# Ending the first tile's attention before the fifth pair begins, and queueing phi behind the preceding pair's minima

## The chip, the cores and the metric

The kernel runs on 1 core of a Trainium2 chip. The metric is device time in microseconds (us) of one execution, lower is better. The engines are PE (matrix products and transposes), DVE (VectorE), ACT (ScalarE), POOL (GpSimd) and SP (which issues the transfers). Each works through its own instructions strictly in order; an instruction waits at the head of its engine until what it needs is there.

## The reference

Attention with a memory branch, then two feed-forward layers, all in float32:

```python
scores = scale * q @ k.T                    # B=4, H=8, S=576, D=64, causal
a = softmax(scores);  local = a @ v
q_p = phi(q)                                # phi(x) = max(x, 0) + min(exp(x), 1)
mem_out = (q_p @ M_prev) / (q_p @ z_prev + 1e-6)
x = g * mem_out + (1 - g) * local           # g = sigmoid(beta), one value a head
x = x.reshape(2304, 512)
h = x @ w_in;  x = (h * sigmoid(1.702 * h)) @ w_out     # 512 -> 2048 -> 512
h = x @ w_in2; x = (h * clip(h + 3, 0, 6) / 6) @ w_out2
```

The feed-forward weights come as 64-bit floats and are turned into 32-bit ones on the chip.

## The kernel before

**Tiles and pairs.** The 2304 tokens are six tiles of 384 columns (`TILES`). Tile 0 is the first 384 rows of batch 0, tile 1 those of batch 1, tile 2 the last 192 rows of both, and so on. The eight heads go two at a time: a tile of one batch has four *pairs* (`NP` = 4), so pairs 0 to 3 make tile 0 and pairs 4 to 7 tile 1.

**Attention of a pair** has three parts. `scores(i)` multiplies q by k into PSUM (names `s`); behind it DVE takes the masked row minima (`masked_min`, L484), ACT the exponentials (`expo`, L489, names `p`), DVE the reciprocals of the row sums (L492, L493) and POOL scales the rows (`norm`, L497). `turn(i)` transposes p on PE (L439, names `t`) and ACT copies the result out (L584, names `pt`). `weigh(i)` multiplies by v (names `o`) and ACT copies the result into the tile's columns `x0` to `x3` (L736), one for each pair. Beside it goes the memory branch: `mem_prep(i)` makes phi of q (ACT L652, DVE L654 and L655), `mem_read(i)` multiplies it by the memory matrix (PE L409, names `mem`) and DVE scales that (L676 to L680, names `mw`, `mo`).

**The pipeline.** `attention` (L440 to L778) is one loop over steps: step i emits the scores of pair i, the transposes of pair i-1 and the product with v of pair i-2. A step therefore holds work of three pairs. The first steps run ahead of everything else with eight PSUM banks (the *prelude*, L864 to L871) until `attention` reports that tile 0 is complete, which it does in step 5. Pairs 4 and 5 belong to tile 1 but their scores are in that prelude. After it `pump` (L827, rate at L887) emits the steps of the next tile's attention between the matmuls of the feed-forward layer, with three banks.

**Feed-forward, layer 0, tile 0.** A tile has 16 blocks f = 0 to 15 (`moe`, L298): four products h (L342), a tanh on ACT (L281) and a product on DVE (L283, result `g`), and four products y (L313) of the same block one block later. Tile 0 takes its weights as whole float32 (`r0` to `r15`); later tiles split them in two (L344 to L347, L314 to L317).

**Weight conversion** (`conv_w`, L168). For each `r{f}`: DVE shift (L186), DVE xor (L191), ACT L195, for some f an absolute value (DVE L199 or ACT L197), ACT L201 and DVE L206, whose result h(f) and y(f) read. `KQ` sets how early in the prelude the first two conversions are emitted (L870).

**What sets the order.** A scheduler orders each engine's instructions from the order in which they are written, within the dependencies; the first instruction of a conversion is kept at its written place (L190), and a conversion follows the DVE and ACT work of an earlier feed-forward block (`after_gates`, L133). The queues of PE, DVE and ACT are thus fixed when the program is built.

Of the kernel before, what the change touches and what calls it, by code (L numbers as in the profile page):

```python
# [12 lines left out]
ALU = mybir.AluOpType  # L13
# [5 lines left out]
NP = H // 2  # L19
# [2 lines left out]
N0, N1 = 384, 192  # L22
NT = 384
PRE = 2
KQ = 39
CR = 8.5
OFF = 3
PG0 = (0.85, 0.55)
PG1 = 0.86
TB = 3  # L30
PB = 6
# [33 lines left out]
BIG = 3.4028234e38  # L65
MZ = 132
TILES = [
    [(0, 0)],
    [(1, 0)],
    [(0, 1), (1, 1)],  # L70
    [(2, 0)],
    [(3, 0)],
    [(2, 1), (3, 1)],
]
# [30 lines left out]
def attention_moe_kernel(ctx: ExitStack, tc: tile.TileContext, qk0, sk0, sk1, vm0, vm1, bb, w1, w2, out):  # L105
    nc = tc.nc
    PE, ACT, DVE, POOL, SP = nc.tensor, nc.scalar, nc.vector, nc.gpsimd, nc.sync
# [332 lines left out]

    def attention(ap):
        qk, vm, pp, pt, phi, mo = {}, {}, {}, {}, {}, {}
        gens, made = {}, {}
        norms = [0, 0]

        t4 = ap.tile([128, 2, 64], F32, tag="t4", bufs=1, name="t4")
# [26 lines left out]
        def load_vm(i):  # L473
            if not 0 <= i < NPAIR:
                return
            ti, si, b, g, p, _ = pairs[i]
            t = ap.tile([128, 5 * 128 + MZ], F32, tag="vm", bufs=2, name="vm")
            nv = (3, 5)[g]
            move(2, out=t[:, 0:nv * 128 + MZ], in_=(vm0, vm1)[g][b, p])
            vm[i] = (t[:, MZ:MZ + nv * 128].rearrange("p (j c) -> p j c", j=nv), t[:, 0:130])  # L480

        def masked_min(o, m, init, out):

            DVE.tensor_tensor_reduce(  # L484
                out=o, in0=o, in1=m, scale=-SCALE, scalar=init, op0=ALU.add, op1=ALU.min, accum_out=out
            )

# [14 lines left out]
        def scores(i):  # L502

            ti, si, b, g, p, _ = pairs[i]
            norms[1] = ti
            q, k = qk[i]
            st = ap.tile([128, 12], F32, tag="st", name="st")
            mx, su = st[:, 0:6], st[:, 6:12]

            def product(banks, blocks):  # L510

                mm = in_a_run(free(banks[0]) + free(banks[1]))
                for o0, o1, c0 in blocks:
                    for a in range(2):
                        h = slice(64 * a, 64 * a + 64)
                        mm(
                            banks[a][:, o0:o1], lhsT=q[h, c0:c0 + 128], rhs=k[h, 0:o1 - o0], start=True, stop=True
                        )

            def soft(s, cols, dst, c):  # L520

                jobs = [(a, c0, c1, c + a * len(cols) + x) for a in range(2) for x, (c0, c1) in enumerate(cols)]
                yield
                for a, c0, c1, k in jobs:
                    masked_min(s[a][:, c0:c1], mask[:, 512 - (c1 - c0):512], BIG, mx[:, k:k + 1])
                yield
                for a, c0, c1, k in jobs:
                    d = expo(dst[a][:, c0:c1], s[a][:, c0:c1], mx[:, k:k + 1], su[:, k:k + 1])
                    if c1 == cols[-1][1]:
                        has_read(s[a], d)  # L530
                yield
                inverse(su[:, c:c + len(jobs)])
                yield
                for a, c0, c1, k in jobs:
                    norm(dst[a][:, c0:c1], su[:, k:k + 1], omg[:, 2 * p + a:2 * p + a + 1])

            pp[i] = []
            if g == 0:
                parts = (((0, 128, 0), (128, 384, 128)), ((0, 384, 256),))
            else:  # L540
                parts = (((0, 512, 0),),)
            t = [[ap.tile([128, 512], F32, tag="p", bufs=PB, name="p") for _ in parts] for _ in range(2)]
            pp[i] = [tuple(x) for x in t]
            c = 0
            for x, blocks in enumerate(parts):
                s = [bank("s") for _ in range(2)]
                product(s, blocks)
                start(("s", i, x), soft(s, [(o0, o1) for o0, o1, _ in blocks], [t[a][x] for a in range(2)], c))
                c += 2 * len(blocks)
                yield  # L550
            if g == 1:
                t = ap.tile([128, 512], F32, tag="p", bufs=PB, name="p4")
                t2 = ap.tile([128, 64], F32, tag="p5", name="p5")
                pp[i].append((t, t2))
                s, s2 = bank("s4"), bank("s5")
                mm = in_a_run(free(s) + free(s2))
                for o, c0, c1 in ((s, 0, 512), (s2[:, 0:64], 512, 576)):
                    for a in range(2):
                        h = slice(64 * a, 64 * a + 64)
                        mm(o[h], lhsT=q[h, 128:N1], rhs=k[h, c0:c1], start=True, stop=True)  # L560

                def soft4(s=s, s2=s2, t=t, t2=t2):
                    yield
                    masked_min(s, mask[:, 0:1].to_broadcast([128, 512]), BIG, mx[:, 2:3])
                    masked_min(s2[:, 0:64], mask4, mx[:, 2:3], mx[:, 3:4])
                    yield
                    has_read(s, expo(t, s, mx[:, 3:4], su[:, 2:3]))
                    has_read(s2, expo(t2, s2[:, 0:64], mx[:, 3:4], su[:, 3:4]))
                    yield
                    DVE.tensor_tensor(out=su[:, 2:3], in0=su[:, 2:3], in1=su[:, 3:4], op=ALU.add)  # L570
                    inverse(su[:, 2:3])
                    yield
                    norm(t, su[:, 2:3], omp[:, p:p + 1])
                    norm(t2, su[:, 2:3], omp[:, p:p + 1])

                start(("s", i, 2), soft4())
                yield
# [66 lines left out]
        def mem_prep(i):  # L644

            ti, si, b, g, p, _ = pairs[i]
            n = (N0, N1)[g]
            e = ap.tile([128, NT], F32, tag="tmp", bufs=TB, name="phi")
            phi[i] = e
            r = qk.pop(i)[0]  # L650
            yield
            ACT.activation(out=e[:, 0:n], in_=r, func=AF.Exp)  # L652
            yield
            DVE.tensor_scalar(out=e[:, 0:n], in0=e[:, 0:n], scalar1=1.0, scalar2=None, op0=ALU.min)  # L654
            DVE.scalar_tensor_tensor(out=e[:, 0:n], in0=r, scalar=0.0, in1=e[:, 0:n], op0=ALU.max, op1=ALU.add)  # L655

        def mem_read(i):
# [88 lines left out]
                yield None  # L746

        def has(i):
            return 0 <= i < NPAIR

        nil = iter(())
        load_qk(0)
# [1 line left out]
        load_qk(1)  # L754
        load_w(W0)
        gs, gt, gw = {}, {}, {}
        for i in range(NPAIR + 2):
            if has(i):
                gs[i] = scores(i)
            if has(i - 1):  # L760
                gt[i - 1] = turn(i - 1)
            if has(i - 2):
                gw[i - 2] = weigh(i - 2)
            s, t, w = gs.pop(i, nil), gt.pop(i - 1, nil), gw.pop(i - 2, nil)
            for gen, n in (
                (s, 1), (t, 1), (w, 1), (s, 1), (t, 1), (w, 9), (s, 1), (t, 1), (s, 9),
            ):
                yield from chunks(gen, n)
            if has(i):
                start(("p", i), mem_prep(i))  # L770
                load_qk(i + 2)
            if has(i - 2) and pairs[i - 2][5]:
                need(("x", i - 2))
                yield pairs[i - 2][0]
            load_vm(i)
            if has(i - 1):
                yield from mem_read(i - 1)
            yield from chunks(t, 9)  # L778


    with ExitStack():
# [80 lines left out]
        with tc.tile_pool(name="ap", bufs=2) as ap:  # L862
            temps[:] = [ap, TWB[0]]
            att = state["att"] = attention(ap)  # L864
            banks[0] = 8
            for k, mark in enumerate(att):
                chains.step()
                if mark is not None:
                    break
                convert_to(min(PRE, int(PRE * k / KQ) + K0))  # L870
            convert_to(PRE)  # L871
            banks[0] = 3
            phase["behind"] = lambda: marks[-1 - SLACK] if len(marks) > SLACK else None
            qi, ti = 0, 0
            for layer, t, f in stream:
                if t != ti:
                    ti, qi = t, 0
                    if t == LAST:
                        break
                if qi == 0:  # L880
                    state["emitted"], state["done"] = 0, False
                qi += 1
                if ti == 0:
                    convert_to(min(NF, PRE + 1 + int(qi / CR)))
                if ti < 2 and 128 * ti + qi >= S2:
                    part_to(1 + (128 * ti + qi - S2) // SR)
                pump((qi - OFF) / (PG0[min(ti, 1)] * 128 / 36 if TILES[ti + 1][0][1] == 0 else PG1 * 128 / 57))  # L887

        with tc.tile_pool(name="x2p", bufs=2) as x2p:
            state["pool"] = x2p  # L890
# [68 lines left out]
```

## Time and profile before

| | |
|---|---|
| median of 3 runs | 1048.41 us (1048.25 to 1051.59) |
| span of the profiled execution | 1049.0 us |
| time of the profiled execution beside its span | none is recorded of its own; the span is 0.6 us over the median |
| PE busy | 1029.6 us, 98% |
| DVE, ACT, POOL busy | 467.4, 510.2, 293.7 us |

PE, DVE, ACT and POOL are the engines; a busy share is over the whole span. In a row of the timeline the first number is the start in us, the second the time that the row's instructions took together, and the bracket at the end is how long the engine stood idle just before, and which instruction released it. The prelude lasts to 44.5 us, tile 0 of the feed-forward layer to 162.2 us.

### The profile page before, as it was taken

How to read it: one execution, taken by the hardware profiler on the slowest of the kernel's cores; microseconds unless marked ns; L12 is line 12 of the kernel's file. 1: busy time of each engine (PE TensorE's matmuls, PEld its weight loads, DVE VectorE, ACT ScalarE, POOL GpSimd, SP SyncE). 2: the span in 40 equal slices, each digit the busy share in tenths (PEclk: the TensorE clock that was granted, in tenths of full speed). 3: DMA queues.
4: the chain of work that ended last, by engine and by line, in shares of the span. 5: the costliest groups of instructions: out<-in, count | busy, mean ns of one | idle time of the engine just before them, and what ended most of it. 6: DMA issues, size and time to landing. Idle time of an engine off the chain costs nothing.

```text
span 1049.0 us, 16113 instructions
## 1 busy us (share of the span) xinstructions
PE 1029.6 (98%) x6025; PEld 914.9 (87%) x6025; DVE 467.4 (45%) x1153; ACT 510.2 (49%) x1110; POOL 293.7 (28%) x346
## 2 busy tenths in 40 slices
PE   8899999999999999999999999999999999999998
PEld 5555558988888888898889999999999999999998
DVE  6977766666533343433443697971121211211110
ACT  5876746545634454433333778883232332332322
POOL 4522112333333332322222241332222222222221
PEclk8999999999999999999999999999999999999999
DMA  5864314332211021111100784001010010000000
GB/s 185 277 232 137 136 55 153 129 118 65 81 42 36 26 67 46 31 31 61 47 16 16 271 302 173 18 11 52 1 46 16 10 52 1 31 31 1 31 1 30
DMA packets 33885, 80.27 MB, mean 77 GB/s; under 512 B 4112, under 2 KB 13328, under 8 KB 33808
## 3 DMA queue, kind: packets, MB, share of 16 engines
q1 hardware_dynamic: 33808, 79.25, 22.4%
q8 instruction: 47, 0.77, 0.3%
q14 instruction: 30, 0.25, 0.1%
HBM read 61.41 MB, written 9.44 MB: 68 GB/s over the span
## 4 chain that ended last, share of the span: by engine, by line
PE 86%; DVE 6%; ACT 5%; issue 2%; DMA 1%; SPq 0%; POOL 0%; DVEq 0%; ACTq 0%
PE y L315 11%; PE h L344 11%; PE y L317 11%; PE y L316 11%; PE h L347 11%; PE h L346 11%; PE s L424 5%; PE o L424 5%; PE h L342 3%; PE y L313 3%; PE t L439 3%; ACT p L489 2%; PE mem L409 1%; DVE s L484 1%; DVE r L191 1%
## 5 line engine op out<-in xcount | busy, mean ns | idle before, releaser
L295 POOL TENSOR_TENSOR g<-t,g 128x384 fp32r<-128x384 f32 x173 | 185.2, 1071 | 481.6 <-ACT g L292 433.0
L344 PE MATMUL h<-xs,w 128*128 128x384 f32 x704 | 241.4, 343 | 1.6 <-DVE t L283 0.9
L315 PE MATMUL y<-g,w 128*128 128x384 f32 x704 | 237.2, 337 | 0.5 <-ACT g L292 0.5
L316 PE MATMUL y<-g,w 128*128 128x384 f32 x704 | 236.3, 336 | 0.0
L346 PE MATMUL h<-xs,w 128*128 128x384 f32 x704 | 236.0, 335 | 0.3 <-DVE w L228 0.3
L347 PE MATMUL h<-xs,w 128*128 128x384 f32 x704 | 236.0, 336 | 0.0
L317 PE MATMUL y<-g,w 128*128 128x384 f32 x704 | 223.6, 338 | 0.0
L287 DVE SCALAR_TENSOR_TENSOR t<-t,h 128x384 f32<-128x384 f32 x96 | 53.0, 553 | 275.5 <-ACT t L285 275.4
L344 PEld LDWEIGHTS h<-xs,w 128*128 128x128 f32 x704 | 132.3, 188 | 10.1 <-issue 5.2
L285 ACT ACTIVATE t<-h,three 128x384 f32<-128x384 f32 x96 | 55.6, 580 | 170.2 <-PE h L347 170.1
L497 POOL TENSOR_SCALAR p<-p,st,omg 128x128 f32<-128x128 f32 (+3 forms) x128 | 85.8, 683 | 186.3 <-DVE st L493 122.1
L317 PEld LDWEIGHTS y<-g,w 128*128 128x128 f32 x704 | 130.4, 188 | 5.6 <-issue 4.9
L315 PEld LDWEIGHTS y<-g,w 128*128 128x128 f32 x704 | 132.2, 188 | 2.8 <-issue 1.3
L292 ACT CAST g<-t 128x384 fp32r<-128x384 f32 x176 | 90.1, 514 | 90.9 <-DVE t L287 49.3
L346 PEld LDWEIGHTS h<-xs,w 128*128 128x128 f32 x704 | 132.4, 188 | 0.7 <-DVE w L228 0.5
L316 PEld LDWEIGHTS y<-g,w 128*128 128x128 f32 x704 | 132.2, 188 | 0.7 <-issue 0.5
L347 PEld LDWEIGHTS h<-xs,w 128*128 128x128 f32 x704 | 132.2, 188 | 0.5 <-issue 0.5
L489 ACT ACTIVATE p<-s,st 128x512 f32<-128x512 f32 (+4 forms) x160 | 82.5, 524 | 73.3 <-DVE st L484 61.5
L484 DVE CUSTOM_DVE_ANT_0 s<-s,mask 128x128 f32<-128x128 f32 (+3 forms) x144 | 72.3, 529 | 72.1 <-PE s L424 71.3
L281 ACT ACTIVATE t<-h 128x384 f32<-128x384 f32 x96 | 46.8, 491 | 66.8 <-PE h L347 54.7
L424 PE MATMUL s<-qk 64*128 64x256 f32 (+5 forms) x384 | 70.2, 461 | 3.3 <-ACT p L489 2.4
L283 DVE SCALAR_TENSOR_TENSOR t<-t,h 128x384 f32<-128x384 f32 x80 | 44.0, 552 | 62.5 <-ACT t L281 59.2
(82 smaller groups left out, 1111.9 us busy)
## 6 DMA issues: line engine op xcount, KB each, us to landing
r<-in_w_dram SPq DMA_DIRECT2D x64, 512.0 KB, 6.3
wt<-r SPq DMA_DIRECT2D x32, 256.0 KB, 2.3
vm<-in_vm_dram SPq DMA_DIRECT2D x16, 386.0 KB, 3.0
qk<-in_qk_dram SPq DMA_DIRECT2D x16, 384.0 KB, 3.5
qk<-in_sk_dram SPq DMA_DIRECT2D x32, 192.0 KB, 3.8
x2d<-yo SPq DMA_DIRECT2D x24, 192.0 KB, 2.0
xr<-x2d SPq DMA_DIRECT2D x24, 192.0 KB, 3.0
out_dram<-yo SPq DMA_DIRECT2D x24, 192.0 KB, 1.9
```

Source lines behind the costliest of these rows:

```text
L292: gated["ACT"].append(ACT.copy(out=g[:, 0], in_=t).ins)
L295: d = {"DVE": DVE, "POOL": POOL}[e].tensor_tensor(out=g[:, 1], in0=t, in1=f32(g[:, 0]), op=ALU.subtract)
L315: PE.matmul(ys[d], lhsT=w[:, 0, o:o + 128], rhs=g[:, 0], start=(f == 0), stop=False)
L316: PE.matmul(ys[d], lhsT=w[:, 1, o:o + 128], rhs=g[:, 0], start=False, stop=False)
L317: PE.matmul(ys[d], lhsT=w[:, 0, o:o + 128], rhs=g[:, 1], start=False, stop=(f == NF - 1))
L344: PE.matmul(h, lhsT=w[:, 0, c:c + 128], rhs=x[:, 0], start=first, stop=False)
L346: PE.matmul(h, lhsT=w[:, 1, c:c + 128], rhs=x[:, 0], start=False, stop=False)
L347: PE.matmul(h, lhsT=w[:, 0, c:c + 128], rhs=x[:, 1], start=False, stop=last)
L424: ins = PE.matmul(out, **args).ins
L484: DVE.tensor_tensor_reduce(out=o, in0=o, in1=m, scale=-SCALE, scalar=init, op0=ALU.add, op1=ALU.min, accum_out=out)
L489: return ACT.activation(out=dst, in_=o, func=AF.Exp, scale=-1.0, bias=m, accum_out=s)
L497: (DVE, POOL)[e[norms[0] % len(e)]].tensor_scalar(out=dst, in0=dst, scalar1=s, scalar2=w, op0=ALU.mult, op1=ALU.mult)
```

## The change

Five edits. The loop runs over two ranges of pairs, (0, 4) and (4, end), and `has(i)` is true only inside the running range: the first range is taken to its end (step 5 emits only the end of pair 3), then step 4 of the second range begins with pair 4. `load_vm(i)` is called only for pairs of the range. `masked_min` returns its instruction, the last one of each pair is kept in `masked`, and for pairs of the first tile (i < `NP`) DVE's first phi operation is issued after the last minimum of pair i-1. `KQ` goes from 39 to 30. The pump's rate in tile 0 goes from 36 to 43 yields a tile (`MARKS`), since more of tile 1's attention now lies inside it.

```diff
-KQ = 39
+KQ = 30
...
+MARKS = (43, 36)
...
         def masked_min(o, m, init, out):
 
-            DVE.tensor_tensor_reduce(
+            return DVE.tensor_tensor_reduce(
...
-                    masked_min(s[a][:, c0:c1], mask[:, 512 - (c1 - c0):512], BIG, mx[:, k:k + 1])
+                    masked[i] = masked_min(s[a][:, c0:c1], mask[:, 512 - (c1 - c0):512], BIG, mx[:, k:k + 1])
...
             ACT.activation(out=e[:, 0:n], in_=r, func=AF.Exp)
             yield
-            DVE.tensor_scalar(out=e[:, 0:n], in0=e[:, 0:n], scalar1=1.0, scalar2=None, op0=ALU.min)
+            first = masked.get(i - 1) if i < NP else None
+            with tc.issue_after(first.ins) if first is not None else ExitStack():
+                DVE.tensor_scalar(out=e[:, 0:n], in0=e[:, 0:n], scalar1=1.0, scalar2=None, op0=ALU.min)
             DVE.scalar_tensor_tensor(out=e[:, 0:n], in0=r, scalar=0.0, in1=e[:, 0:n], op0=ALU.max, op1=ALU.add)
...
         def has(i):
-            return 0 <= i < NPAIR
+            return lo <= i < hi
...
-        for i in range(NPAIR + 2):
+        runs = ((0, NP), (NP, NPAIR))
+        for lo, hi, i in ((lo, hi, i) for lo, hi in runs for i in range(lo, hi + 2)):
...
-            load_vm(i)
+            if has(i):
+                load_vm(i)
...
-                pump((qi - OFF) / (PG0[min(ti, 1)] * 128 / 36 if TILES[ti + 1][0][1] == 0 else PG1 * 128 / 57))
+                pump((qi - OFF) / (PG0[min(ti, 1)] * 128 / MARKS[min(ti, 1)] if TILES[ti + 1][0][1] == 0 else PG1 * 128 / 57))
```

Line numbers in the changed file lie 1 to 5 higher (L191 is now L192, L342 now L343, L654 now L657). The orders of the engines show where instructions went. Numbers behind a name only tell buffers apart, and differ between the two builds.

**First place: DVE at the start of the program.** `phi_229` is phi of pair 1, `s_137` and `s_148` are scores of pair 0, `gall`, `omg`, `omp` the gates of the heads. Before:

```order
L814 RECIPROCAL gall_107<-gall_107 128x8
L654 TENSOR_SCALAR phi_229<-phi_229 128x384
L815 TENSOR_SCALAR omg_108<-gall_107 128x8
L655 SCALAR_TENSOR_TENSOR phi_229<-qk_127,phi_229 128x384
L821 COPY omp_109<-omg_108 64x4 x2
L484 ISA s_137,st_132<-s_137,mask_93 128x128
```

Now:

```order
L819 RECIPROCAL gall_107<-gall_107 128x8
L820 TENSOR_SCALAR omg_108<-gall_107 128x8
L826 COPY omp_109<-omg_108 64x4 x2
L485 ISA s_137,st_132<-s_137,mask_93 128x128
...
L485 ISA s_148,st_132<-s_148,mask_93 128x384
L485 ISA st_132 128x1
L657 TENSOR_SCALAR phi_229<-phi_229 128x384
L658 SCALAR_TENSOR_TENSOR phi_229<-qk_127,phi_229 128x384
```

Both phi operations of pair 1 moved from ahead of pair 0's minima to behind them.

**Second place: PE ahead of h(f7) in tile 0.** `h_956` and `h_917` are h of block 7, `y0` the y of block 6. Before:

```order
L424 MATMUL s_979<-qk_785 128x512
L424 MATMUL s_980<-qk_785 128x512
L439 MATMUL t_1003<-ident_88,p_826 128x128 x2
L439 MATMUL t_1003<-ident_88,p_827 128x128
L313 MATMUL y0_658<-g_918,r6_728 128x384
...
L313 MATMUL y3_661<-g_918,r6_728 128x384
L342 MATMUL h_956<-x0_289,r7_774 128x384
```

Now:

```order
L314 MATMUL y3_574<-g_873,r6_656 128x384
L440 MATMUL t_806<-ident_88,p_591 128x128 x2
L440 MATMUL t_806<-ident_88,p_592 128x128
L410 MATMUL mem_823<-vm_679,phi_676 128x130 x3
L440 MATMUL t_846<-ident_88,p_591 128x128
L440 MATMUL t_846<-ident_88,p_592 128x128 x2
L425 MATMUL s_862<-qk_677 128x128
...
L440 MATMUL t_885<-ident_88,p_715 128x128
L425 MATMUL o_904<-ident_88,mo_827 128x128 x3
...
L425 MATMUL o_904<-pt_805,vm_679 64x128
L343 MATMUL h_917<-x0_289,r7_708 128x384
```

Between y of block 6 and h of block 7 there now stand a pair's memory product, half of its successor's scores, nine transposes and a product with v.

**Third place: DVE at the same point.** `mw_828` and `mo_827` scale that memory product `mem_823`, `r7_708` is the weight that h(f7) reads, `g_918` and `g_873` the g of block 6. Before:

```order
L186 TENSOR_SCALAR r7_774<-r7_774 128x1024
...
L191 SCALAR_TENSOR_TENSOR r7_774<-r7_774 128x1024
...
L283 SCALAR_TENSOR_TENSOR g_918<-t_919,h_903 128x384
...
L206 SCALAR_TENSOR_TENSOR r7_774<-r7_774 128x2x512
```

Now:

```order
L284 SCALAR_TENSOR_TENSOR g_873<-t_874,h_852 128x384
L493 TENSOR_SCALAR st_713<-st_713 128x2
L494 RECIPROCAL st_713<-st_713 128x2
L679 TENSOR_SCALAR mw_828<-mem_823 128x6
...
L683 TENSOR_TENSOR mo_827<-mem_823,mw_828 128x384
L187 TENSOR_SCALAR r7_708<-r7_708 128x1024
L657 TENSOR_SCALAR phi_965<-phi_965 128x384
L192 SCALAR_TENSOR_TENSOR r7_708<-r7_708 128x1024
...
L200 TENSOR_SCALAR r7_708<-r7_708 128x1024
...
L207 SCALAR_TENSOR_TENSOR r7_708<-r7_708 128x2x512
```

Before, the first operations on r7 stood ahead of g of block 6; now the whole conversion stands behind it, and behind the memory product that PE does after y of block 6.

## Rows read from the trace of the kernel before

**Rows 1.** The page: busy times, and the chain that ended last, by engine

```profile
PE 1029.6 (98%) x6025; PEld 914.9 (87%) x6025; DVE 467.4 (45%) x1153; ACT 510.2 (49%) x1110; POOL 293.7 (28%) x346
...
PE 86%; DVE 6%; ACT 5%; issue 2%; DMA 1%; SPq 0%; POOL 0%; DVEq 0%; ACTq 0%
```

**Rows 2.** Busy time by stretch: start:end, length, each engine, granted clock (PEclk), DMA

```profile
0.00:44.50 44.50, 37.55 (x231) 24.80 (x231) 32.75 (x139) 32.70 (x108) 20.13 (x47) 0.92 0.62 213
...
51.90:162.20 110.30, 107.09 (x441) 62.76 (x441) 80.33 (x167) 72.09 (x129) 22.35 (x24) 0.98 0.41 142
162.20:1049.00 886.80, 878.75 (x5323) 823.92 (x5320) 347.44 (x833) 400.67 (x867) 247.30 (x274) 1.00 0.18 59
```

**Rows 3.** Timeline of PE: blocks that were waited for, with the idle time before

```profile
10.30 1.56 PE L424 MATMUL s<-qk 64*128 64x384 f32 x4 [2.36 <-ACT p L489]
...
51.86 2.85 PE L342 MATMUL h<-x,r 128*128 128x384 f32 x8 [0.18 <-DVE g L283]
...
72.50 2.85 PE L342 MATMUL h<-x,r 128*128 128x384 f32 x8 [0.70 <-DVE g L283]
...
140.16 4.51 PE L342 MATMUL h<-x,r 128*128 128x384 f32 x8 [2.46 <-DVE g L283]
```

**Rows 4.** Busy time and granted clock in the stretches behind two of those waits

```profile
10.00:15.00 5.00, 4.33 (x16) 2.75 (x17) 3.63 (x19) 3.17 (x15) 3.25 (x6) 0.54 0.60 199
...
140.00:145.00 5.00, 4.84 (x10) 2.80 (x11) 2.56 (x10) 1.74 (x5) 1.52 (x2) 0.66 0.00 0
```

**Rows 5.** Timeline of DVE at the start: phi of pair 1 and the first minimum

```profile
7.13 0.36 DVE L654 TENSOR_SCALAR phi<-phi 128x384 f32<-128x384 f32 x1 [1.64 <-ACT phi L652]
...
8.37 0.30 DVE L484 CUSTOM_DVE_ANT_0 s<-s,mask 128x128 f32<-128x128 f32 x1
```

**Rows 6.** Timeline of ACT at the start: the gates' last copy and the first exponential

```profile
7.20 0.19 ACT L818 COPY gall<-gall 64x8 f32<-64x8 f32 x1
9.33 0.37 ACT L489 ACTIVATE p<-s,st 128x128 f32<-128x128 f32 x1 [1.94 <-DVE st L484]
```

**Rows 7.** Timeline of PE in the prelude: one pair's pieces, back to back

```profile
26.33 0.49 PE L424 MATMUL o<-ident,mo 128*128 128x128 f32 x3
...
28.20 0.88 PE L439 MATMUL t<-ident,p 128*128 128x128 f32 x6
28.91 0.83 PE L409 MATMUL mem<-vm,phi 128*128 128x130 f32 x6
29.58 0.49 PE L439 MATMUL t<-ident,p 128*128 128x128 f32 x3
30.00 0.93 PE L424 MATMUL s<-qk 64*128 64x128 f32 x8
```

**Rows 8.** Timeline of POOL: the six row scalings of a pair, early and beside conversions

```profile
11.66 3.25 POOL L497 TENSOR_SCALAR p<-p,st,omg 128x128 f32<-128x128 f32 x6 [9.41 <-ACT p L489]
...
42.79 5.66 POOL L497 TENSOR_SCALAR p<-p,st,omg 128x128 f32<-128x128 f32 x6 [2.50 <-ACT x L736]
```

**Rows 9.** Groups of DVE by form, 0 to 165 us: count, busy us, mean ns, idle before

```profile
L191 DVE SCALAR_TENSOR_TENSOR r<-r 128x1024 int32<-128x1024 int32 x16 | 21.0, 1313 | 0.2
L206 DVE SCALAR_TENSOR_TENSOR r<-r 128x1024 f32<-128x1024 f32 x16 | 19.7, 1230 | 12.4 <-ACT r L201 12.4
L186 DVE TENSOR_SCALAR r<-r 128x1024 int32<-128x1024 int32 x16 | 11.1, 691 | 0.0
...
L680 DVE TENSOR_TENSOR mo<-mem,mw 128x384 f32<-128x384 f32 x8 | 4.4, 554 | 0.1
...
L678 DVE TENSOR_TENSOR mw<-mw,gall 128x6 f32<-128x6 f32 x8 | 1.5, 193 | 0.2
```

**Rows 10.** Groups of ACT by form, 0 to 165 us: the two conversion steps

```profile
L195 ACT ACTIVATE r<-r,step_up 128x1024 f32<-128x1024 f32 x16 | 20.5, 1279 | 13.7 <-DVE r L191 13.6
L201 ACT ACTIVATE r<-r,step_down 128x1024 f32<-128x1024 f32 x16 | 19.9, 1247 | 0.2
```

**Rows 11.** Timeline of ACT: the first cast of a split weight

```profile
57.32 1.14 ACT L225 CAST w<-wt 128x512 fp32r<-128x512 f32 x2 [0.80 <-PE y L313]
```

More of the change, by code (lines that the diff above doesn't have):

```diff
@@ L442, in attention @@
         qk, vm, pp, pt, phi, mo = {}, {}, {}, {}, {}, {}
-        gens, made = {}, {}
+        gens, made, masked = {}, {}, {}
         norms = [0, 0]
```

## The prediction

> **What bounds the kernel now.** I read the page first, for the engine that is never idle: PE is busy for 98% of the span, and 86% of the chain that ended last is PE's [rows 1]. Next to it DVE and ACT are half idle, taken over the whole. Then the same by stretch [rows 2], because an average hides the start: from 162 us on PE is idle for 8 us in 887, but in the prelude it is idle for 7 of 44.5 us while DVE and ACT are busy for 33 each, and in tile 0 of the feed-forward layer it is idle for 3.2 of 110. So PE's work sets the time nearly everywhere. A change in the order of the work can give or take only idle time of PE, and slow clock, in the first 162 us. The orders of the engines agree again early in tile 1, so I add nothing behind it. Third, the waits of PE in that part [rows 3]: 2.36 us before pair 1's second scores, 0.70 and 2.46 us for g of a block (DVE) in tile 0. Fourth, the granted clock behind them [rows 4]: 0.54 in the 5 us from 10 us, 0.66 in those from 140 us. The block h at 140.16 took 4.51 us where the same eight matmuls took 2.85 [rows 3]: 1.66 us of clock, on top of the 2.46 of waiting.
>
> **The base.** The profiled execution's span is 1049.0 us, 0.6 over the median of 1048.41. The sum is made against 1049.0, and the forecast is lowered by 0.6.
>
> **Part 1: phi of pair 1 behind pair 0's minima.** Before, DVE stands 1.64 us waiting for ACT's phi, then does it, and the first minimum starts at 8.37 [rows 5]. Without that wait, phi's first operation (0.36) and its second (of the kind and size of L680, 0.55 [rows 9]), the minimum moves by up to 2.55, to about 6.0 with the gates' copies still ahead of it. The first exponential cannot follow at once: ACT is still at the gates' last copy until 7.20 + 0.19 = 7.39 [rows 6]. It moves from 9.33 to 7.40, 1.9 us earlier. The 2.36 us that PE waits for these exponentials [rows 3] shrink by as much. The moved phi falls behind the minima, where ACT is the later of the two engines; I count 0.1. **Gain 1.8 us by pair 2's scores.** What is late next is ACT itself: it was 33 us busy in this stretch [rows 2].
>
> **Part 2: the prelude ends with pair 3.** Nothing of PE's work is added or removed. Moved behind h(f1) are, in PE time, the scores of pair 5 and half of pair 6's, three halves: each took 0.93 with a tail that the next block covers, so 0.85, and 3 × 0.85 = 2.55; fifteen transposes, six in 28.91 - 28.20 = 0.71, so 1.8; one memory product, 29.58 - 28.91 = 0.67; one product with v, 28.20 - 26.33 = 1.87 [rows 7]. Together 6.9. With the same idle time, h(f1) would start at 51.86 - 6.9 = 45.0 [rows 3].
> The idle time is not the same. In the old prelude, while the last step of pair 3 waits for an exponential, a scaling or a copy, PE has pair 4's and 5's work. In the new one, pair 3's chain (minima, exponentials, reciprocals, POOL's scalings, transposes, copies, product with v) has nothing behind it, and the conversions of r0 and r1 now stand among its links on DVE and ACT: 0.69 + 1.31 + 1.23 on DVE [rows 9] and 1.28 + 1.25 on ACT [rows 10] for each. I follow it from pair 3's scores, 1.8 earlier than before: the conversions' steps included, the last exponential ends at about 31.8, and the last six scalings start at 31.5 (an estimate from the rows' durations, good to 1 us). These took 3.25 us early in the program and 5.66 beside conversions [rows 8], so I take the slow row: transposes done about 37.7, the first h about the same, h(f1) about 45.6. With the fast row it is 45.0. So the drain eats the gain of part 1, and **the prelude as a whole costs 0.6** (0 with the fast row; -1.8 if the drain costs nothing; +1.5 if ACT falls behind).
> The Trainium skill's page "GPSIMD Engine Reference", section "Specifications", says that GpSimd's memory interfaces are shared with VectorE, with contention against VectorE instructions that have two inputs in SBUF. L191 and L206 are such instructions; by that rule the slow row holds in the drain and the sum is as below, without it 0.6 lower. The two rows agree with it.
>
> **Part 3: tile 0 of the feed-forward layer.** Removed: the waits at 72.50 (0.70) and 140.16 (2.46 and 1.66 of clock) [rows 3]. At the second, only a memory product and half of a pair's scores stood between h of blocks 12 and 13; now y of block 11 and a pair's last transposes stand there too, as many matmuls as in an h block (2.85) and more. **Gain 4.8.**
> New waits, read from the places in the orders:
> - Ahead of h(f7) (second and third place): DVE must scale `mem` before it starts on r7. From the end of that memory product: three small operations of 0.19 and L680 (1.1), L186 (0.65), phi's first (0.3), L191 (1.3), ACT L195 (1.28) and L201 (1.22), L206 (1.2) = 7.05, each a little under its row, since they overlap [rows 5, 9, 10]. PE has beside it three transposes 0.35, scores 0.85, three transposes 0.33, a product with v 1.87 [rows 7] = 3.4. **Stall 3.6.** It is one wait as long as those at 10.30 and 140.16, so the clock may fall for one h block, 1.7. I count none of it, as the next stall would end at the same time.
> - Ahead of y(f7): r8's L191 on DVE and two conversion steps on ACT stand ahead of the tanh of block 7. DVE gets to them about 1 us after h(f7) starts, as it waits for exponentials first; then 1.31 + 1.28 + 1.25, tanh and g about 0.5 each, 4.85 in all [rows 9, 10]. PE has h 2.7, half a pair's scores 0.85, three transposes 0.4 [rows 3, 7]. 1.0 + 4.85 - 3.95 = **1.9.**
> - Ahead of h(f11): behind g(f10) DVE has r11's L191, a scaling of `mem`, r12's L186 and L191, both phi operations of a pair, and only then r11's L206: 6.2 against 4.2 to 5.5 of PE's work. **1.8**, the upper part because the memory product itself is late.
> - Ahead of h(f4): a split weight's cast on ACT waits for y of block 0 (before: 0.80 of waiting, 1.14 of work [rows 11]) and holds up what is behind it: **0.55**.
> - Start of tile 1: 0 to 0.8; I take 0.
> Sum 7.85. Bounds: below, 3.6 alone, since the other three each hang on a difference of 1 to 2 us between two long chains; above, 7.85 + 1.7 + 0.8 = 10.4.
> `load_vm` for pairs outside the range, `KQ` and the pump's rate cost nothing themselves; they act through these places. SP's queue moves a pair's `vm` load later, but the queue has slack there (data needed two steps on).
>
> **Sum.** 1049.0 + 0.6 - 4.8 + 7.85 = 1052.7; less 0.6: **1052.1 us.** A measurement of this kernel tells apart about 0.3%, 3.1 us: faster is below 1045.3, slower above 1051.55.
>
> **The rivals.**
> *A, the forecast* (0.42): the stall at h(f7) and most of the three others are there. 1050.5 to 1054.
> *B, faster* (0.18): the start decides. Pair 0's chain starts 1.9 earlier, and if the drain's scalings run at the fast row beside pair 3's last minima, the gain of 1.8 stays; DVE and ACT then enter tile 0 with less in arrears, the old waits are gone, and of the new ones only 3.6 is left. 1049.0 - 1.8 - 4.8 + 3.6 - 0.6 = 1045.4. For it: PE's largest early wait is exactly for these exponentials [rows 3]. Against it: L206's slow neighbours on POOL [rows 8], and DVE and ACT at 33 us of 44.5 [rows 2]. It decides at h(f1): before 43.5 us means B.
> *C, same* (0.25): the prelude is even, the stall at h(f7) takes the place of the one at 140.16, and the rest is hidden as the chains start a little earlier: 1049.0 + 0.6 - 4.8 + 3.6 + 0.55 - 0.6 = 1048.4. For it: before, L206 as a whole waited 12.4 us for ACT in 16 conversions [rows 9], and PE felt 3.2 of that.
> *D, slower still* (0.15): waits of 2 us and more cost clock as well [rows 4]. After h(f7) it is absorbed, but after h(f11) it is not (1.66), and tile 1 starts late (0.8): 1052.1 + 2.5 = 1054.6. For it: both long waits of before were followed by a low clock. Against: 0.70 cost none.
> The Trainium skill's "Trainium Architecture — The Big Picture", section "What this means for kernel authors", says that PE runs at 1.2 or 2.4 GHz depending on recent activity; that is D's rule, and the low clock at both long waits agrees with it. By it alone the time would be D's.
>
> **How the numbers follow.** Slower: three quarters of A, all of D: 0.46. Same: most of C and a quarter of A: 0.35. Faster: B and a little of C: 0.19. The range takes in B's time and D's with the upper bounds of part 3 beyond it: 1045.0 to 1056.5. A's own range is 1050.5 to 1054.
>
> **What would show it.** Right: the first exponential near 7.4; the wait at 10.30 under 0.7; h(f1) at 45.0 to 45.6; a wait for DVE ahead of h of block 7 of 3 us or more; none at h of block 13; PE's idle time in the first 160 us larger by 2 to 5 us. Wrong: h(f1) before 43.5 (the drain is free), or no wait ahead of h(f7) over 2 us (DVE reached r7 before that memory product), or differences behind 170 us.

## The result, and the profile after

| | before | after |
|---|---|---|
| median, same comparison | 1048.54 us | 1063.80 us (1061.99 to 1064.32) |
| ratio, 95% interval | | 1.0137 [1.0122, 1.0153] |
| span of the profiled execution | 1049.0 | 1061.3 |
| PE busy up to the end | 1029.6 | 1032.6 |

The change makes the kernel slower by 1.4%. I had forecast slower, but by 0.35%, and the range ended at 1056.5: the direction was right, the size was not.

The profiled execution of the kernel before is one of its slower ones: in every execution with both on record the time lies 1.7 to 3.7 us above the span, so a span of 1049.0 goes with a time of 1050.7 or more. The two profiles therefore differ by 12.3 us, where the ratio says 14.4; the account below is of the 12.3.

First the page of the changed kernel, busy times and the chain that ended last [rows 1]:

```profile
PE 1032.6 (97%) x6025; PEld 915.0 (86%) x6025; DVE 467.3 (44%) x1153; ACT 510.4 (48%) x1110; POOL 292.6 (28%) x346
...
PE 82%; DVE 8%; ACT 6%; issue 2%; DMA 1%; POOL 0%; SPq 0%; DVEq 0%; ACTq 0%
```

The counts of instructions are the same. Of the 12.3 us, 3.0 are PE being busy longer for the same matmuls, 9.3 are PE idle.

Where does it lie? The views by stretch are cut at the start of h of block 1, called h(f1) from here on, and at the first h of tile 1. At the second cut both kernels have done nearly the same matmuls; at the first the changed one has done 56 fewer, the 6.9 us that the prediction moved behind it. Columns: start:end, length, PE, PEld, DVE, ACT, POOL busy (and count), granted clock, DMA share, GB/s. Before:

```profile
0.00:51.86 51.86, 43.72 (x265) 28.16 (x266) 39.62 (x155) 37.40 (x116) 24.08 (x49) 0.93 0.68 229
51.86:162.19 110.33, 107.12 (x440) 62.79 (x441) 80.36 (x167) 72.12 (x129) 22.34 (x24) 0.98 0.41 142
```

After:

```profile
0.00:25.00 25.00, 20.10 (x110) 12.79 (x110) 17.16 (x73) 15.78 (x53) 10.49 (x29) 0.93 0.56 193
25.00:35.00 10.00, 6.84 (x45) 4.64 (x45) 8.92 (x30) 7.75 (x22) 3.38 (x5) 0.93 0.98 353
35.00:45.00 10.00, 7.88 (x34) 4.38 (x30) 7.09 (x10) 6.02 (x9) 5.78 (x4) 0.73 0.99 382
45.00:50.57 5.57, 4.12 (x27) 1.88 (x26) 3.04 (x11) 3.34 (x10) 0.00 (x0) 1.00 0.55 192
50.57:175.27 124.70, 115.53 (x500) 67.74 (x501) 84.73 (x200) 77.81 (x156) 27.53 (x36) 0.99 0.34 115
```

The prelude ends at 50.57 instead of 51.86, but 6.9 us of its PE work now lie behind it: against 45.0 it is **5.6 late**. Tile 0 takes 124.70 instead of 110.33 + 6.9 = 117.2: **7.5 more**. From tile 1 on the span is 0.8 shorter. 5.6 + 7.5 - 0.8 = 12.3.

The timeline of PE at the end of the prelude, after:

```profile
29.92 0.55 PE L440 MATMUL t<-ident,p 128*128 128x128 f32 x3 [0.95 <-ACT pt L585]
31.48 0.91 PE L410 MATMUL mem<-vm,phi 128*128 128x130 f32 x6 [1.01 <-DVE mo L683]
33.57 0.48 PE L440 MATMUL t<-ident,p 128*128 128x128 f32 x1 [1.19 <-POOL p L498]
...
34.62 2.63 PE L425 MATMUL o<-pt,vm 128*64 128x384 f32 x12
...
38.67 0.55 PE L440 MATMUL t<-ident,p 128*128 128x128 f32 x3 [0.50 <-POOL p L498]
40.84 0.90 PE L440 MATMUL t<-ident,p 128*128 128x128 f32 x3 [1.62 <-POOL p L498]
41.53 3.20 PE L343 MATMUL h<-x,r 128*128 128x384 f32 x6
...
49.44 0.92 PE L425 MATMUL s<-qk 64*128 64x384 f32 x4 [1.24 <-ACT p L490]
50.57 2.85 PE L343 MATMUL h<-x,r 128*128 128x384 f32 x8 [0.22 <-DVE g L284]
```

Seven waits in 21 us. The first two stand at pair 2's last transposes and at pair 3's memory product (for a copy and a scaling of pair 2), the next three are for pair 3's scalings, one is for pair 4's exponentials and the last, 0.22, for g of block 0. Between them matmuls ran at a lowered clock: the product with v at 34.62 took 2.63 us, where a pair's twelve took 1.52 in the kernel before:

```profile
26.75 1.52 PE L424 MATMUL o<-pt,vm 128*64 128x384 f32 x12
```

POOL's and DVE's rows for the wait of 1.19:

```profile
33.07 7.71 POOL L498 TENSOR_SCALAR p<-p,st,omg 128x128 f32<-128x128 f32 x6 [5.51 <-DVE mw L681]
```

```profile
32.42 0.16 DVE L679 TENSOR_SCALAR mw<-mem 128x6 f32<-128x6 f32 x1 [0.94 <-PE mem L410]
32.50 0.16 DVE L493 TENSOR_SCALAR st<-st 128x4 f32<-128x4 f32 x1
32.62 0.19 DVE L680 RECIPROCAL mw<-mw 128x6 f32<-128x6 f32 x1
32.73 0.15 DVE L494 RECIPROCAL st<-st 128x4 f32<-128x4 f32 x1
```

The reciprocals (`st`, L494) that the scalings need stand behind the scaling of a memory product, for which DVE waited 0.94 us on PE; POOL starts at 33.07, and its six scalings took 7.71 us, more than either figure of [rows 8].

The waits of PE in tile 0, after; blocks h start at 71.05 (f4), 102.38 (f7), 139.84 (f11), and 108.37 is y(f7):

```profile
71.05 2.85 PE L343 MATMUL h<-x,r 128*128 128x384 f32 x8 [0.73 <-DVE g L284]
...
96.60 0.93 PE L425 MATMUL s<-qk 64*128 64x128 f32 x8 [1.00 <-ACT phi L653]
98.57 0.55 PE L425 MATMUL o<-ident,mo 128*128 128x128 f32 x3 [0.57 <-ACT pt L585]
102.38 2.85 PE L343 MATMUL h<-x,r 128*128 128x384 f32 x8 [1.82 <-DVE r L207]
108.37 4.54 PE L314 MATMUL y<-g,r 128*128 128x384 f32 x8 [1.81 <-DVE g L284]
...
139.84 2.85 PE L343 MATMUL h<-x,r 128*128 128x384 f32 x8 [1.46 <-DVE r L207]
```

Of the waits of [rows 3] in tile 0 the one at h(f13) is gone, the one at h(f4) stayed (0.70 before, 0.73 now), and the others are new. At the start of the program the first minimum moved from 8.37 [rows 5] to 6.17, the first exponential from 9.33 [rows 6] to 7.14, the wait of 2.36 [rows 3] went to 0.57.

### The profile page after: what moved, and what is told of

Its sections match the earlier page's. It is cut to its first block, busy times and chain, and to the rows that moved or that the text cites. A ratio compares the mean times of both kernels' runs of the same rounds, so it can differ in the third digit from the quotient of the medians.

```text
span 1061.3 us, 16122 instructions
## 1 busy us (share of the span) xinstructions
PE 1032.6 (97%) x6025; PEld 915.0 (86%) x6025; DVE 467.3 (44%) x1153; ACT 510.4 (48%) x1110; POOL 292.6 (28%) x346
## 4 chain that ended last, share of the span: by engine, by line
PE 82%; DVE 8%; ACT 6%; issue 2%; DMA 1%; POOL 0%; SPq 0%; DVEq 0%; ACTq 0%
PE y L316 11%; PE y L317 10%; PE y L318 10%; PE h L345 10%; PE h L347 10%; PE h L348 10%; PE o L425 5%; PE s L425 5%; PE h L343 3%; PE t L440 3%; PE y L314 2%; ACT p L490 1%; DVE r L192 1%; PE mem L410 1%; DVE r L187 1%
```

## The experiments

"Idle in tile 0" is PE's idle time from h(f1) to the first h of tile 1 (3.2 before, 9.2 after). Ratios are to the kernel before, in brackets the 95% interval. The cut at tile 1 hides what a run shifts behind it, so where that matters PE's idle time from the start of the program to tile 1 is given too: 11.3 before, 20.8 after.

**The parts alone.** Phi's new place in the kernel before, without the split:

```diff
-            DVE.tensor_scalar(out=e[:, 0:n], in0=e[:, 0:n], scalar1=1.0, scalar2=None, op0=ALU.min)
+            first = masked.get(i - 1) if i < NP else None
+            with tc.issue_after(first.ins) if first is not None else ExitStack():
+                DVE.tensor_scalar(out=e[:, 0:n], in0=e[:, 0:n], scalar1=1.0, scalar2=None, op0=ALU.min)
```

> The kernel before with phi queued behind the preceding pair's minima, and nothing else of the change. Theory (the loss is the split into two ranges; phi's place is worth its 1.8 us at the start): first exponential at about 7.4, the wait of PE at 10.3 shrinks from 2.36 to under 0.7, time 1045.5 to 1048 us, a gain of 0.5 to 2.5. Rival (phi's place itself delays the memory products and the chains behind them): 1050 us or more, with waits of PE for mo or phi in the prelude.

Ratio 0.9989 [0.9978, 1.0000]: the interval reaches 1, so a gain in the whole is not clear of the noise. In the profiled execution h(f1) is at 49.83, 2.0 earlier. Phi's place is not the loss.

```profile
0.00:49.83 49.83, 41.81 (x266) 26.49 (x266) 40.01 (x155) 37.53 (x116) 24.48 (x49) 1.00 0.71 240
```

PE's idle time up to h(f1) is 8.0 here against 8.1 before: the 2.0 us are matmuls that ran faster, at a granted clock of 1.00 against 0.93. The trace has the old long wait too, and this time the block behind it ran at full clock:

```profile
138.16 2.85 PE L342 MATMUL h<-x,r 128*128 128x384 f32 x8 [2.48 <-DVE g L283]
```

The changed kernel without phi's place:

```diff
-            first = masked.get(i - 1) if i < NP else None
+            first = None
```

> The changed kernel without phi's new place; the split into two ranges, KQ = 30 and the pump's rate stay. Theory: slower than the changed kernel by up to 2 us or equal to it, 1062 to 1066 us, with h of block 1 at 50 us or later. Rival (phi's place is the cause): near the kernel before, 1046 to 1052 us.

1.0124 [1.0106, 1.0142], h(f1) at 53.10. The split, with its `KQ` and its rate, carries the whole loss. Phi's 2.5 us at h(f1) hardly show in the end: spans 1062.2 and 1061.3.

`KQ` and the pump's rate, each put back:

```diff
-KQ = 30
+KQ = 39
```

> The changed kernel with KQ back at 39, so that the first conversions are written later in the prelude. Theory (pair 3's chain has nothing behind it, whatever stands beside it): 1060 to 1065 us; what the last scalings gain, the first h pays, as it waits for r0. Rival (the conversions within pair 3's chain are the cost of the prelude): h of block 1 at 46 us or earlier instead of 50.6, and 1057 to 1060 us.

1.0111 [1.0092, 1.0130]. The prelude's end did change as the rival said: with the conversions later, pair 3's six scalings started 3.2 us sooner and took 3.56 us instead of 7.71, and h(f1) came at 44.81.

```profile
29.84 3.56 POOL L498 TENSOR_SCALAR p<-p,st,omg 128x128 f32<-128x128 f32 x6 [3.42 <-ACT pt L585]
```

```profile
44.81 4.29 PE L343 MATMUL h<-x,r 128*128 128x384 f32 x8 [3.25 <-DVE g L284]
```

But PE waited 3.25 us for g just before, that block took 4.29, and idle in tile 0 rose to 10.6. PE's idle time up to tile 1 is 20.4, hardly below 20.8: the waits moved, and of the 2.5 us of span that went, 2.4 are matmuls that ran faster.

```diff
-MARKS = (43, 36)
+MARKS = (36, 36)
```

> The changed kernel with the pump's rate in tile 0 back at 36. Theory (the waits ahead of h of blocks 7 and 11 and y of block 7 come from tile 1's four pairs, all of them now in tile 0): 1061 to 1066 us, as what is emitted later in tile 0 has to be done before tile 1. Rival (the higher rate crowds tile 0): the waits of PE in tile 0 fall from 9 us to 4, time 1057 to 1060 us.

1.0108 [1.0088, 1.0128], idle in tile 0 7.8, not the rival's 4; and less of the attention was done by tile 1, behind which the span is 4.8 longer. The constants tuned for the split are worth 2 to 3 us each at most (the intervals overlap the changed kernel's), not the loss. Both put back together were not run.

**The end of the prelude.** No conversions in it, scalings on another engine, or one more pair in the first range:

```diff
-KQ = 30
+KQ = 300
```

> The changed kernel with KQ = 300: all weight conversions are written behind the first tile's attention, none inside it. Theory (pair 3's chain has no other PE work beside it; the conversions only decide who waits): the six last scalings take under 4 us instead of 7.7 and the last transposes end by 33, but h of block 0 then waits for r0, which takes 5.5 to 6 us from its first step, so h of block 1 is at 44 to 48 us and the time 1057 to 1062 us. Rival (the conversions inside the chain are what the prelude lost): h of block 1 before 44 us, 1055 us or less.

1.0078 [1.0053, 1.0104]. The first h comes at 39.38 and y(f0) now stands ahead of h(f1), at 49.69. The scalings took 3.23, under 4 as the theory had it. Half a per cent came back, within the theory's range of times, though h(f1) is outside its 44 to 48; the rival's 44 was not reached. PE's idle time up to tile 1 is 20.1.

```diff
-NR = ((1,), (1,), (1,), (1,), (1,), (1,))
+NR = ((1,) * 18 + (0,) * 6, (1,), (1,), (1,), (1,), (1,))
```

> The changed kernel with pair 3's six row scalings on DVE instead of POOL (about 0.4 us each there, 2.3 in all). Theory (POOL's scalings beside conversions, 7.7 us for six, are the last link of the drain): the wait of PE for POOL ahead of the last transposes, 1.19 + 0.50 + 1.62, goes, h of block 1 moves from 50.6 to 46 to 48, time 2 to 4 us less, 1058 to 1061. Rival (the drain is bound by DVE's and ACT's own queues; POOL is only the last name): h of block 1 within 1 us of 50.6, time unchanged.

1.0093 [1.0071, 1.0114], h(f1) at 47.62. PE's waits for POOL at the end are gone, 3 us of 5.6 came back. But PE then waits 2.05 for the exponentials of pair 4:

```profile
46.66 0.92 PE L425 MATMUL s<-qk 64*128 64x384 f32 x4 [2.05 <-ACT p L490]
```

```diff
-        runs = ((0, NP), (NP, NPAIR))
+        runs = ((0, NP + 1), (NP + 1, NPAIR))
...
-KQ = 30
+KQ = 35
...
-MARKS = (43, 36)
+MARKS = (40, 36)
```

> The changed kernel with the first range one pair longer, (0, 5): pair 4's scores and transposes stand beside pair 3's chain again, pairs 5 and on begin in tile 0 (KQ = 35, pump rate 40, between the two kernels). Theory (what is missing is PE work beside pair 3's chain): of the 5.6 us that h of block 1 is late against its moved work, 4 or more come back, time 1049 to 1056 us. Rival (the loss sits in tile 0, where a restarted pipeline follows): 1058 us or more.

1.0081 [1.0057, 1.0104], 1057.73 us, between the two expectations. The two stretches, cut at h(f1) and tile 1:

```profile
0.00:46.77 46.77, 39.40 (x250) 25.88 (x251) 38.03 (x134) 34.31 (x102) 19.91 (x43) 0.96 0.68 245
46.77:170.41 123.64, 114.03 (x465) 65.25 (x464) 84.24 (x192) 75.85 (x145) 30.24 (x30) 0.97 0.38 130
```

With pair 4 beside pair 3, PE's idle time in the prelude is 7.4, below the 8.1 of before (after: 11.6). The run changes `KQ` and the rate as well, but later conversions alone left PE's idle time up to tile 1 at 20.4 and 20.1; here it is 17.0. So what the prelude lost in idle time was PE work beside one pair's chain, while the place of the conversions decided where PE waits. Tile 0 is as bad as ever, 9.6 idle: the two costs are separate.

**Tile 0.** Conversions written sooner, a third range, and conversions cut down:

```diff
-CR = 8.5
+CR = 7.5
```

> The changed kernel with the conversions of tile 0 written sooner (CR = 7.5 quarters a weight instead of 8.5). Theory (the waits ahead of h of blocks 7 and 11 are late conversions, queued on DVE behind the scaling of a memory product): these two waits, 1.8 and 1.5 us, and that ahead of y of block 7 shrink by half or more, 2 to 4 us less, 1058 to 1061; the drain is untouched. Rival (the waits come from the dense attention work and only move to other blocks): idle time of PE in tile 0 stays 8 to 10 us, time within 1.5 us of the changed kernel's.

1.0123 [1.0100, 1.0146], idle 8.3. The rival: the wait at h(f7) went, that at h(f11) shrank to 0.35, and others came, 3.07 for an exponential of phi, at the scores just ahead of h(f7), the longest. Not foreseen: h(f1) came at 47.62, 3.0 earlier, and the time did not follow.

```diff
-        runs = ((0, NP), (NP, NPAIR))
+        runs = ((0, NP), (NP, 2 * NP), (2 * NP, NPAIR))
...
-MARKS = (43, 36)
+MARKS = (36, 43)
```

> The changed kernel with a third range: tile 1's pairs too are taken to their end before tile 2's pairs begin, so tile 0 holds four pairs from start to end and nothing of pairs 8 and 9 (rate 36 in tile 0, 43 in tile 1). Theory A (tile 0's new waits come from how much attention is packed into it: two pairs' scores and one's transposes more than before): PE's idle time between h of block 1 and tile 1 falls from 9 to 6 us or less. Theory B (they come from the pipeline that starts anew inside tile 0, with pair 4's chain at its head and the conversions behind it): it stays at 8 to 10 us. The total is no clean measure, as tile 1 now has its own end and start of a range: 1058 to 1068 us.

1.0113 [1.0098, 1.0129], idle 7.2, with 46 fewer matmuls done by tile 1: between the two, it decides nothing.

```diff
-            DVE.scalar_tensor_tensor(
-                out=lo, in0=hi, scalar=3, in1=lo, op0=ALU.logical_shift_left, op1=ALU.bitwise_xor
-            )
...
+            thin = layer == 0 and f > PRE
+            if not thin:
+                DVE.scalar_tensor_tensor(
+                    out=lo, in0=hi, scalar=3, in1=lo, op0=ALU.logical_shift_left, op1=ALU.bitwise_xor
+                )
             yield
-            ACT.activation(out=f32(hi), in_=f32(hi), func=AF.Identity, bias=step_up[:, 0:1])
+            if not thin:
+                ACT.activation(out=f32(hi), in_=f32(hi), func=AF.Identity, bias=step_up[:, 0:1])
-            if f % ABS[z][1] < ABS[z][0]:
+            if thin:
+                pass
+            elif f % ABS[z][1] < ABS[z][0]:
...
-            ACT.activation(out=f32(hi), in_=f32(hi), func=AF.Sign, bias=step_down[:, 0:1])
+            if not thin:
+                ACT.activation(out=f32(hi), in_=f32(hi), func=AF.Sign, bias=step_down[:, 0:1])
```

> The changed kernel with the conversions of r3 to r15 cut down: DVE's shift and DVE's last product stay, the xor and ACT's steps (and the absolute value) are left out, so these weights hold other numbers. About 2.0 us of DVE and 2.5 to 3.6 of ACT less for each of 13 blocks. Theory (the waits in tile 0 are conversion chains queued behind attention): PE's idle time between h of block 1 and tile 1 falls from 9.2 to 4 us or less. Rival (the waits are the attention's own chains, scores to exponentials to transposes): it stays at 7 us or more.

> The control: the kernel before with the same conversions cut down in the same way (r3 to r15 hold other numbers). Theory: the waits of 0.7 and 2.5 us for g, behind conversions, go, and PE's idle time in tile 0 falls from 3.2 to 1 us or less. Rival: it stays at 2 us or more.

Spans 1050.7 and 1042.5 (one execution each). Tile 0, first of the changed kernel cut down, then of the kernel before cut down:

```profile
49.38:164.19 114.81, 112.29 (x497) 66.57 (x497) 68.39 (x180) 43.30 (x124) 28.70 (x36) 1.00 0.37 125
```

```profile
50.62:154.19 103.57, 103.57 (x431) 61.08 (x431) 62.96 (x141) 35.57 (x92) 21.56 (x22) 1.00 0.40 143
```

Idle falls from 9.2 to 2.5, and from 3.2 to 0. The waits in tile 0 are conversions queued among attention on DVE and ACT, in both kernels. That those of the changed one are longer because more attention stands there is an argument; the run with three ranges was to test it and did not.

Both costs taken out at once, and the control for it:

> The changed kernel with both found costs taken out at once: the conversions of r3 to r15 cut down (those weights hold other numbers) and pair 3's scalings on DVE. If the drain's scalings and the conversions in tile 0 are the whole loss, what is left against the kernel before with phi's new place and the same cut conversions is 3 us or less. Rival (the split costs something of its own, PE work that no order covers): 5 us or more are left.

> The control for the run beside it: the kernel before with phi's new place and the same conversions cut down. Expected 2 us below the control without phi's new place (span 1042.5), so 1040 to 1042, with no idle time of PE between h of block 1 and tile 1.

The edits are those above, put together. Ratios 1.0004 [0.9988, 1.0020] and 0.9946 [0.9933, 0.9958], spans 1050.3 and 1043.0: **7.3 are left** (6.1 by the ratios), the rival's case. The control missed its 1040 to 1042: its h(f1) is at 50.73, against 50.62 without phi's new place, as 1.9 us less of idle time met 2.0 us more of PE time. First the prelude of the one, and 5 us within it, then the prelude of the control:

```profile
0.00:49.05 49.05, 38.70 (x210) 24.26 (x210) 37.73 (x128) 32.88 (x93) 12.02 (x31) 0.86 0.75 274
...
35.00:40.00 5.00, 5.00 (x25) 3.16 (x24) 5.00 (x12) 2.60 (x5) 0.00 (x0) 0.52 1.02 396
```

```profile
0.00:50.73 50.73, 43.15 (x266) 27.68 (x266) 40.23 (x155) 37.47 (x116) 24.51 (x49) 0.93 0.70 235
```

With POOL out of the chain, h(f1) is still at 49.05, against 50.73 - 6.9 = 43.8: 5.2 of the 7.3. It is 2.8 of idle time (10.35 to 7.58) and 2.4 of slower matmuls (38.70 to 43.15 - 6.9): right behind the waits at 30 to 34 us PE worked five microseconds without a pause at a granted clock of 0.52. Tile 0 takes 4.3 more than the control's and the 6.9 together, 2.5 of it idle time, and from tile 1 on the span is 2.3 shorter, as the control does 13 more matmuls there. So POOL's scalings were the last link and not the cause; in one order taking them out gave 3 us at h(f1), in another 0.3. Five pairs in the first range together with the cut conversions, which would take out both costs as they are now understood, was not run.

**A version that beats both.** Phi's place without the split, and conversions sooner:

```diff
-CR = 8.5
+CR = 7.5
```

> A candidate: the kernel before with phi's new place (no split), and the conversions of tile 0 written sooner (CR = 7.5 instead of 8.5), so that r13 is ready when h of block 13 comes. Theory: the wait of 2.5 us ahead of h of block 13 goes or halves, PE's idle time in tile 0 falls from 3.2 to 1 to 2 us, time 1045 to 1048 us, a little below phi alone. Rival (the wait moves to another block): idle time in tile 0 stays at 3 us or more, time as with phi alone.

0.9982 [0.9972, 0.9991], 1.9 us below the kernel before: small, but the interval lies below 1, so it beats both kernels. Against phi alone (0.9989) it is not told apart. The long wait at h(f13) is gone, but idle in tile 0 is 3.5, with 1.04 ahead of y(f2) the longest: the rival was right about where the time goes.

## Why the prediction was wrong

*Part 1 was right in its times, and partly by luck.* The first exponential came 2.2 us earlier for 1.9 forecast, and pair 2's first scores 2.1 earlier (15.64 for 17.73) for 1.8. But PE did not wait less: up to those scores it was idle for 4.4 us before, 4.3 with phi alone and 4.8 in the changed kernel. The wait of 2.36 for exponentials shrank, and waits for POOL's scalings grew from 0.6 to 2.8 in its place (with phi alone); it was POOL that PE waited for next, not ACT. What was gained is slow clock, 0.54 behind the wait before [rows 4] and 1.00 in the same stretch of both later profiles.

*Part 2 failed; it is the larger half of the miss.* Its step "the prelude as a whole costs 0.6", which took the idle time as before and added one slow link, became 5.6: idle time 3.5 more, and slow matmuls 2.1 more. I followed pair 3's chain link by link, and three things were too small. The scalings did not start at 31.5 but at 33.07; 0.94 of that is DVE waiting for PE ahead of their reciprocals. Six of them took 7.71 instead of 5.66. Behind them came a link that I had left out of the price, pair 4's first scores and their exponentials, 1.24 with nothing beside them. And I gave the drain, the stretch in which pair 3's chain runs to its end, no clock: PE's matmuls up to h(f1) took 4.0 us more than at full clock (38.93 against 41.81 - 6.9 in the run with phi alone, whose clock was 1.00), against 1.9 before. Of the 4.0, 1.0 lies ahead of 25.4 us, before the drain, and 3.1 in it. This is not one unlucky execution: the eight profiles with two ranges or three, four pairs in the first and `KQ` = 30, show 37.5 to 41.2 us of PE time there, where full clock gives 34.9.

The run with five pairs in the first range shows the cause of the idle time: PE work beside the chain; with it, the idle time was back to 7.4. Why the scalings were slow and late is another matter: it hung on the conversions beside them, as they took 3.56 and 3.23 us where these were written later.

The bounds of this part, -1.8 to +1.5, were too narrow. They came from a drain that costs nothing and from ACT falling behind, and not from the chain as a whole with no cover at all.

The step on `vm` ("the queue has slack there") did not hold in every order either: with the scalings on DVE, PE waited 0.61 us for that load.

*Part 3 had the right places and prices for the waits.* DVE's chain ahead of h(f7) began at 95.31, after 2.12 us of waiting for the memory product, and PE started h(f7) at 102.38, 7.1 later for 7.05 forecast:

```profile
95.31 0.17 DVE L679 TENSOR_SCALAR mw<-mem 128x6 f32<-128x6 f32 x1 [2.12 <-PE mem L410]
```

PE's idle time in it was 3.4 for 3.6, but in three waits, 1.00 and 0.57 for ACT and 1.82 for DVE; the last is below the 2 us that I had named as a sign of being wrong, though the reason given there (DVE at r7 before the product) did not occur. y(f7) 1.9 forecast and 1.81; h(f11) 1.8 and 1.46; h(f4) 0.55 and 0.73; the start of tile 1, taken at 0, 1.04 (0.20 and 0.84); not foreseen were 0.39 and 0.35 at two other blocks. Sum 9.2 for 7.85. The wait at h(f13) went as forecast.

Of the 4.4 us by which tile 0 missed (7.5 for 3.05), 1.3 are waits and the rest is matmuls that ran longer. What failed is "I count none of it" of the clock: y(f7) took 4.54 instead of 2.85, so 1.7. It was there that I had reasoned the loss away, since the next stall "would end at the same time"; the clock fell behind the second stall instead of the first. This 1.7 is no sure price of the wait: without phi's place, the same waits of 1.83 and 1.81 were followed by full clock.

```profile
110.57 2.85 PE L314 MATMUL y<-g,r 128*128 128x384 f32 x8 [1.81 <-DVE g L284]
```

Another 1.4 of PE time has no wait beside it: that run, whose clock in tile 0 was 1.00, shows 113.9 of PE time there against 112.5 (105.57 with phi alone, and the 6.9). Tile 0 is broken into more and shorter pieces, which may be why; no run shows it.

*The base.* I read the span of 1049.0 as 0.6 above the median time. It belongs to a time of 1050.7 or more, with slow clock in two places. What the change removes of that clock is no gain over an execution that has none of it, which may be why the measured loss is 14 to 15 us and that of the profiles 12.3.

*Rival D* was nearest in time, because it was the highest; its clock was to fall behind h(f11), where it did not (2.85 after 1.46), and fell at y(f7) and in the drain, behind waits of 1.81 and less. *B* fell: the drain ate the start's gain and more. *C* fell: the new waits were not hidden.

What stays open: why the clock fell behind some waits and not behind others of the same length, and how much of the 5.6 would go with a better order of the same two ranges. Whether an order exists that covers pair 3's chain with feed-forward work of its own tile was not tried: x3, which h needs last, is that chain's result.

## What to carry to other kernels

A software pipeline that is run to its end before the next one starts shows one item's whole chain to the engine that bounds the kernel. Price it as the sum of that chain's links with nothing beside them, with the queues of all engines between the links, and not as the old idle time plus one link. Before tuning the constants around such a split, run its parts alone: here the small part gained about 0.1%, not clear of the noise, and the large one lost 1.2%. And compare the idle time up to a place that the orders reach with the same work done: h(f1) came 5.8 us earlier with `KQ` back and 3.0 with sooner conversions, and the span fell by 2.5 and 1.1.

## What the runs showed of the hardware that was not expected

The granted clock falls not only behind one long wait. Between 25 and 45 us of the changed kernel no wait is over 1.62 us, yet the granted clock was 0.73 from 35 to 45 us; with scalings on DVE and cut conversions it was 0.52 from 35 to 40 us, while PE was busy throughout, having been busy for 2.31 of the 5 us before. And it is no fixed price of a wait: 2.46 us of waiting at h(f13) were followed by a block of 4.51 us in the kernel before, 2.48 at the same place by one of 2.85 with phi alone; after 1.81 ahead of y(f7) the block took 4.54 in the changed kernel and 2.85 in the one without phi's place. In the first 25 us the changed kernel and the one with phi alone have the same waits up to the place (0.95, 0.30, 0.28, 1.05, 0.21 and 0.95, 0.31, 0.29, 1.04, 0.21 for POOL; the changed kernel shows 0.57 for exponentials besides), and then the same product with v at different clocks:

```profile
17.69 2.56 PE L425 MATMUL o<-pt,vm 128*64 128x384 f32 x12
```

```profile
17.38 1.52 PE L424 MATMUL o<-pt,vm 128*64 128x384 f32 x12
```

One program alone does the same: of 53 executions of the kernel before, 20 had a mean granted clock of 0.998 and spans of 1046.0 to 1047.2 us, the other 33 clocks of 0.993 to 0.997 and spans of 1047.7 to 1050.8.
